# Full-array sums, masks and memory rows with the two attention products apart, and whole accumulators beside the MLP's end, in place of 32-column tiling with adjacent products and single units

## The chip, the core and the metric

The kernel runs on one core of one Trainium2 chip. The core has a matrix engine (TensorE, here PE, with its weight loads listed apart as PEld), VectorE (DVE), ScalarE (ACT), GpSimd (POOL) and SyncE (SP), which issues most DMAs. PE writes only to PSUM, eight banks of 128 x 512 fp32; GpSimd does not read PSUM here. The metric is the device time of one execution in microseconds (us). The kernel before takes 840.97 us (median of 3 runs, 840.32 to 841.74).

## What is computed

`x` is 2048 rows of 512 (bf16). Two branches are mixed by a gate:

```
g = sigmoid((x * gate_w).sum(-1));   out = g * a + (1 - g) * b
b = gelu(layernorm(x) @ w1 + b1) @ w2 + b2            # MLP, 512 -> 1376 -> 512
mem = mem0                                            # 8 rows of 512
for s in range(64):                                   # segments of 32 rows of x
    h = concat([mem, xs])                             # 40 rows
    q, k, v = h @ Wq, h @ Wk, h @ Wv                  # 32 heads of 128
    p = softmax(mask(q @ k.T * scale));  o = (p @ v) @ Wo
    mem, a[s] = o[:8], o[8:]
```

The 8 memory rows that a segment puts out are the first 8 input rows of the next, so the 64 segments are a chain. The other 32 output rows of a segment are not needed by the next one.

## The kernel before, in words

The weights stay in SBUF. First the MLP runs for all 16 tiles of 128 rows: 8 blocks of two tiles, each of 11 chunks of hidden units (88 units `u`); a unit is four 128x256 matmuls (L475) and two 128x512 matmuls (L492) that use the whole 128x128 array. After that comes the loop over 64 segments, four segments (si = 0 to 3) to a tile T.

A segment's 40 rows are split: 32 rows (8 memory rows and 24 rows of x) go through the chain, and the last 8 rows of each of a tile's four segments, the "left" rows, are projected together for a whole tile ahead of time, as side work. Almost every matmul has only 32 rows of output, so four of them are put beside one another in 32-column tiles of the array (`tile_position=(0, 32 * j)`); such a group of four is called a unit here. PE works through a segment in this order, which is the order of the code, since the schedule is manual and every engine takes its instructions in program order:

1. QK: five accumulators in banks of `ring` (L210), 80 matmuls, evacuated by a DVE transpose into `Tt` (L216) and a cast by ACT or POOL (L666).
2. V, first half (L221), then scores (L388, L392) mixed with the second half of V, then the exponentials on ACT (L682, L683).
3. `sums` for the memory rows: a block-diagonal matrix of ones `BO` times E, in 32-column tiles (L365, 8 matmuls). DVE takes the reciprocal (L689) and the product `Pm` (L691).
4. Some units of side work, by `run_fill`.
5. `av` twice (L403, L408), in 32-row tiles of the array (`tile_position=(32 * j, 0)`, 40 matmuls each): the x rows of the segment before (`Px`), and next to it the memory rows of this segment (`Pm`). Both write into the same four banks `U4`.
6. `sums` for the x rows (8 matmuls), one unit of side work, then DVE's second reciprocal (L707).
7. The output projection with Wo (L232) in two halves of 256 columns, 32 matmuls each, into banks `nb` and 6; ACT copies the first half to `wsb`, DVE the second (L727).
8. `mask_mm` for the next segment (L379, 4 matmuls), two units of side work, `mem_out` (L370, 16 matmuls), which transposes the new memory rows, the DVE copy of them into `hT` (L736), and the rest of the side work. Then the next segment's QK, which needs `hT`.

Side work per tile: for si 0 to 2 two accumulators of four units (`left_v`, `left_qk`), for si = 3 `out_units` (two units) and `wo_left` (eight). All side accumulators share bank 5, `out_units` takes bank 6. Evacuations are put into two lists, `act_q` and `dve_q`, and `flush` issues them at set places. `left_qk` is evacuated by an ACT copy into `lt` (L262) and DVE transposes (L266, L270); `out_units` by ACT (L334) and POOL (L335), and SP then issues the output DMA (L336).

For tile 0 the same projections run in `setup()`, beside the last three MLP blocks: the loop over units calls `next(pre, None)` after each unit u, and each call issues one unit of four matmuls.

Of the kernel before, what the change touches and what calls it, by code (L numbers as in the profile page):

```python
# [23 lines left out]
def kernel(ctx, tc, A_x, A_mem0, A_Wq, A_Wk, A_Wv, A_Wo, A_seg_len, B_x, B_w1, B_b1, B_w2, B_b2, gate_w, out):  # L24
    nc = tc.nc
# [149 lines left out]
    pools["nTt"] = 2  # L175

# [18 lines left out]
    def side(shape, dtype=FP32):  # L195
        side_n[0] += 1
        while side_n[0] - 1 in side_todo:
            flush(act_q)
        return bank(5, shape, dtype)
# [52 lines left out]
    def left_qk(T, t, hf):  # L252
# [7 lines left out]
        def ev():  # L260
            lt = pools["sb"].tile([P, 512], BF16, tag="lt", name="lt")
            nc.scalar.copy(out=lt[:], in_=bk[:])  # L262

            def tr():
                if t == 0:
                    nc.vector.transpose(out=QL[T % 2][:, h0:h1, :].rearrange("p h r -> p (h r)"), in_=lt[:])  # L266
                else:
                    for hh in range(h0 // 8, h1 // 8):
                        r0 = 32 * (8 * hh - h0)
                        nc.vector.transpose(out=KL[T % 2][:, :, :, hh, :],  # L270
                                            in_=lt[:, r0:r0 + 256].rearrange("p (g s c) -> p g s c", s=SPT, c=LEFT))
            dve_q.append((None, tr))
        later(act_q, ev, side_k)
        yield

    def left_v(T, vb):
# [7 lines left out]
        def ev():  # L284
            vt = pools["sb"].tile([P, 4, Dh], BF16, tag="lt", name="vt")
# [34 lines left out]
    def out_units(T):  # L320
        ob = bank(6, [P, Dm])
# [7 lines left out]
        o_sb = cw.tile([P, Dm], BF16, tag="o", bufs=1, name="o")  # L329
        if T == NT - 1:  # L330
            nc.vector.scalar_tensor_tensor(out=o_sb[:], in0=ob[:], scalar=g_all[:, T:T + 1], in1=c_all[:, T, :], op0=ALU.mult, op1=ALU.add)
        else:
            of = cw.tile([P, Dm], FP32, tag="Tt", bufs=pools["nTt"], name="of")
            nc.scalar.activation(out=of[:], in_=ob[:], func=ACTF.Copy, scale=g_all[:, T:T + 1])  # L334
            nc.gpsimd.tensor_tensor(out=o_sb[:], in0=of[:], in1=c_all[:, T, :], op=ALU.add)  # L335
        nc.sync.dma_start(out2[T * P:(T + 1) * P, :], o_sb[:])  # L336
# [24 lines left out]

    def sums(o, rhs, start, stop):
        for j in range(4):
            q = slice(32 * j, 32 * j + 32)
            nc.tensor.matmul(o[q], lhsT=BO[:, q], rhs=rhs, start=start, stop=stop, skip_group_check=True, tile_position=(0, 32 * j))  # L365

    def mem_out(aT, wsb):
        for m in range(KC):
            for c in range(4):
                nc.tensor.matmul(aT[32 * c:32 * c + 32, m, :], lhsT=wsb[:, m * P + 32 * c:m * P + 32 * c + 32], rhs=Sel[:, 0:M],  # L370
                                 start=False, stop=True, skip_group_check=True, tile_position=(0, 32 * c))

    def mask_mm():
# [3 lines left out]
        for j in range(4):  # L377
            q = slice(32 * j, 32 * j + 32)
            nc.tensor.matmul(S[q], lhsT=ident[:, q], rhs=MkA[:].unsqueeze(2).to_broadcast([P, 4, 2, EW]),  # L379
                             start=True, stop=True, skip_group_check=True, tile_position=(0, 32 * j))  # L380
# [16 lines left out]
    def av(U, n, s, V, Pt, c_main, c_left, u0, first=True):  # L397

        T, si = divmod(s, SPT)
        for i in range(NG):  # L400
            for j in range(4):
                q = slice(32 * j, 32 * j + 32)
                nc.tensor.matmul(U[j][:, i, :], lhsT=V[q, i, :], rhs=Pt[q, i, c_main:c_main + n],  # L403
                                 start=(first and i == 0), stop=False, skip_group_check=True, tile_position=(32 * j, 0))
# [98 lines left out]
    def setup():  # L503
# [9 lines left out]
        for vb in range(2):  # L513
            yield from left_v(0, vb)
            flush(act_q)
            yield
        for hf in range(2):
            for t in range(2):
                yield from left_qk(0, t, hf)
                flush(act_q)  # L520
                yield
                flush(dve_q)
# [22 lines left out]
    for u in range(NBLK * FC):  # L545
# [34 lines left out]
        if blk >= NBLK - 3:  # L580
# [300 lines left out]
```

## Time and profile before

| what | value |
|---|---|
| median of 3 runs | 840.97 us |
| the profiled execution, its own time | 840.97 us |
| its span, first to last instruction | 839.2 us |
| PE busy | 796.0 us, 95% of the span |
| DVE, ACT, POOL busy | 500.5, 478.8, 246.9 us |
| first QK of segment 0 | 104.37 us |
| first QK of segments 60 and 63 | 780.71 and 813.27 us |
| granted PE clock | 0.999 |

The span is the time from the first to the last instruction; the 1.77 us between it and the execution's time lie outside the instructions. In the timeline a row gives the start and the length in us, then engine, line, operation, output<-inputs, shape and how many instructions are merged. Matmuls overlap, so the distance between the starts of two rows is what a group costs, not its length.

### The profile page before, as it was taken

What the parts mean: (1) busy time and instruction counts of PE and PEld (TensorE: products, weight loads), DVE (VectorE), ACT (ScalarE), POOL (GpSimd) and SP (SyncE); (2) the same over time, 40 slices, a digit from 0 to 9 for tenths busy, and PEclk for the clock granted to TensorE, in tenths of its full rate; (3) what the DMA queues carried; (4) which work ended last, traced back from release to release, by engine and by line L of the source; (5) the groups of instructions that cost most, each with busy time, mean ns of one, the idle gap of its engine ahead of it and who ended that gap; (6) DMA issues with size and microseconds to landing.
All of it is one profiled execution on the core that took longest, in us unless ns stands there. A gap on an engine that the chain in (4) does not pass through costs nothing.

```text
span 839.2 us, 52725 instructions
## 1 busy us (share of the span) xinstructions
PE 796.0 (95%) x24120; PEld 511.4 (61%) x24133; DVE 500.5 (60%) x1036; ACT 478.8 (57%) x1324; POOL 246.9 (29%) x544
## 2 busy tenths in 40 slices
PE   6999989999999999999999999999999999999886
PEld 4665456666666666666666666666666666666554
DVE  5763257565656666665656565656656665656562
ACT  3554556555656556655665565556555556656553
POOL 8000023232333233332323233333233232323321
PEclk9999999999999999999999999999999999999999
DMA  9790300000000010101010100000010101000000
GB/s 320 258 378 26 101 26 14 25 16 15 25 20 26 18 29 10 36 11 36 12 34 5 32 15 23 24 20 27 13 33 11 36 11 33 14 30 4 10 4 24
DMA packets 38230, 37.86 MB, mean 45 GB/s; under 512 B 13545, under 2 KB 36434, under 8 KB 36466
## 3 DMA queue, kind: packets, MB, share of 16 engines
q1 hardware_dynamic: 37874, 34.31, 12.3%
q8 instruction: 190, 3.11, 1.6%
q14 instruction: 38, 0.31, 0.1%
q0 software_dynamic: 128, 0.13, 0.1%
HBM read 26.03 MB, written 6.29 MB: 39 GB/s over the span
## 4 chain that ended last, share of the span: by engine, by line
PE 91%; issue 3%; DVE 2%; DMA 1%; SPq 1%; ACT 1%; POOL 0%; POOLq 0%; DVEq 0%; ACTq 0%
PE b L210 33%; PE b L232 18%; PE b L221 16%; PE b L403 5%; PE hp L475 4%; PE bp L492 4%; PE b L365 3%; PE b L379 2%; PE b L388 2%; PE b L370 1%; PE b L408 1%; DMA Wo_sb<-in_A_x_dram 1%; PE b L392 0%; DVE Tt L216 0%; PE b L323 0%
## 5 line engine op out<-in xcount | busy, mean ns | idle before, releaser
L216 DVE STREAM_TRANSPOSE Tt<-b 128x512 f32<-128x512 f32 (+1 forms) x320 | 180.8, 595 | 77.1 <-PE b L210 63.8
L210 PEld LDWEIGHTS <-hT 128*32 128x32 bf16 x5120 | 133.0, 97 | 106.0 <-DVE hT L736 22.4
L232 PE MATMUL b<-Wo_sb,UTT 128*32 128x256 bf16 (+1 forms) x4736 | 171.6, 285 | 12.5 <-issue 11.9
L232 PEld LDWEIGHTS <-UTT 128*32 128x32 bf16 x4736 | 123.1, 97 | 39.1 <-issue 20.1
L221 PE MATMUL b<-Wv_sb,hT 128*32 128x512 bf16 x2048 | 140.8, 379 | 0.0
L210 PE MATMUL b<-Wq_sb,hT 128*32 128x512 bf16 x2048 | 134.6, 380 | 1.7 <-DVE hT L736 1.6
L210 PE MATMUL b<-Wk_sb,hT 128*32 128x256 bf16 (+1 forms) x3072 | 134.5, 308 | 0.0
L666 ACT CAST KT<-Tt 128x256 bf16<-128x256 f32 (+1 forms) x192 | 87.6, 477 | 49.0 <-DVE Tt L216 48.9
L707 DVE RECIPROCAL R<-b 128x256 f32<-128x256 f32 x64 | 112.5, 1757 | 2.8 <-PE b L365 2.8
L622 POOL TENSOR_TENSOR Px<-E,R 128x256 bf16<-128x256 bf16 x64 | 43.2, 675 | 211.2 <-DVE R L707 211.2
L666 POOL CAST QT<-Tt 128x512 bf16<-128x512 f32 x64 | 39.0, 609 | 220.3 <-DVE Tt L216 220.3
L666 ACT CAST QT<-Tt 128x512 bf16<-128x512 f32 x64 | 39.6, 618 | 81.6 <-DVE Tt L216 81.6
L689 DVE RECIPROCAL R<-b 128x64 f32<-128x64 f32 x64 | 35.7, 557 | 82.2 <-PE b L365 82.2
L631 ACT CAST UTT<-b 128x256 bf16<-128x256 f32 x256 | 78.3, 395 | 6.2 <-PE b L232 6.2
L403 PEld LDWEIGHTS <-V 32*128 32x128 bf16 x4096 | 43.8, 91 | 33.4 <-issue 29.0
L221 PEld LDWEIGHTS <-hT 128*32 128x32 bf16 x2048 | 50.4, 96 | 21.0
L480 ACT ACTIVATE hg<-hp,b_sb 128x256 bf16<-128x256 f32 x80 | 37.7, 473 | 43.0 <-PE hp L475 42.9
L706 ACT CAST UTT<-b 128x64 bf16<-128x64 f32 x128 | 21.0, 215 | 62.9 <-PE b L408 62.7
L475 PE MATMUL hp<-yT,w_sb 128*128 128x256 bf16 (+1 forms) x352 | 54.0, 278 | 2.9 <-ACT hg L480 1.5
L262 ACT CAST lt<-b 128x512 bf16<-128x512 f32 x64 | 37.4, 585 | 32.8 <-PE b L210 13.2
L624 POOL TENSOR_TENSOR racc<-racc,R 128x320 f32<-128x320 f32 x64 | 55.5, 867 | 0.0
L727 ACT CAST wsb<-b 128x256 bf16<-128x256 f32 x66 | 24.6, 372 | 45.2 <-PE b L232 45.2
(113 smaller groups left out, 1134.9 us busy)
## 6 DMA issues: line engine op xcount, KB each, us to landing
Wv_sb<-in_A_Wv_dram SPq DMA_DIRECT2D x4, 1024.0 KB
Wq_sb<-in_A_Wq_dram SPq DMA_DIRECT2D x4, 1024.0 KB
Wk_sb<-in_A_Wk_dram SPq DMA_DIRECT2D x4, 1024.0 KB
Wo_sb<-in_A_Wo_dram SPq DMA_DIRECT2D x2, 2048.0 KB
vd<-vt SPq DMA_DIRECT2D x32, 128.0 KB
vs<-vd SPq DMA_DIRECT2D x256, 16.0 KB
out_dram<-o SPq DMA_DIRECT2D x16, 128.0 KB
Wo_sb<-in_A_x_dram SPq DMA_DIRECT2D x1, 1024.0 KB
```

What stands on the lines that cost most here:

```text
L210: nc.tensor.matmul(bk[32 * j:32 * j + 32, 0:n], lhsT=G[:, kc, :], rhs=W5[t][:, kc, h0:h1, j, :], start=(kc == 0), stop=(kc == KC - 1), til ...
L216: nc.vector.transpose(out=Tt[:, 0:n], in_=bk[:, 0:n])
L221: nc.tensor.matmul(bk[32 * j:32 * j + 32, :], lhsT=G[:, kc, :], rhs=Wv5[:, kc, 4 * vb:4 * vb + 4, j, :], start=(kc == 0), stop=(kc == KC - ...
L232: nc.tensor.matmul(bk[32 * g:32 * g + 32, :], lhsT=ut[:, i, j, c0:c0 + 32], rhs=Wo_sb[:, 4 * i + j, d0:d1], start=(j == 0 and i < 4), stop ...
L403: nc.tensor.matmul(U[j][:, i, :], lhsT=V[q, i, :], rhs=Pt[q, i, c_main:c_main + n], start=(first and i == 0), stop=False, skip_group_check ...
L475: nc.tensor.matmul(hp[:rows, :], lhsT=w1_sb[:, kc, fc * P:fc * P + rows], rhs=yTs[blk][:, kc, :], start=(kc == 0), stop=(kc == KC - 1))
L480: nc.scalar.activation(out=hg_[:rows, :], in_=hp[:rows, :], func=ACTF.Gelu_apprx_tanh, bias=b1_sb[:rows, fc:fc + 1], scale=1.0)
L622: nc.gpsimd.tensor_tensor(out=Px[:, :, 0:32], in0=E[:, :, 16:48], in1=Rr, op=ALU.mult)
L624: nc.gpsimd.tensor_tensor(out=racc[:], in0=racc[:], in1=R[:], op=ALU.add)
L631: nc.scalar.copy(out=UTT[T % 2][:, :, j, c0 + M:c0 + 40], in_=U)
L666: (nc.gpsimd.tensor_copy if bi == 2 else nc.scalar.copy)(out=dst, in_=Tv)
L707: nc.vector.reciprocal(out=R[:, 8 * NG:].rearrange("p (i q) -> p i q", q=32), in_=sr)
```

## The change

- In `setup()` an accumulator's four units are issued at one call, and the MLP's loop makes a call only at every fourth unit u: six accumulators of 16 matmuls in place of 24 calls of 4.
- The `sums`, `mask_mm` and `mem_out` matmuls use the whole array: 2 matmuls for each `sums` (were 8), 1 for the mask (were 4), 4 for `mem_out` (were 16).
- The x rows' product (`av_x`) moves from in front of the memory rows' product to behind the mask, into banks `ne, na, nc_, nb`, where `nb` holds the first half of the output projection until it is evacuated. The memory rows' product has four banks alone.
- `run_fill` is 5 + (si == 3) and then 1 in front of the output projection, and behind it 2 for si == 3 only (were 3 + 2 * (si == 3) + (s == 0), 1, and 2).
- The second half of the output projection goes to bank `nd` instead of 6. DVE copies the first half to `wsb`, ACT the second.
- Side work alternates between two banks, 5 and 6. `left_qk` is transposed by DVE straight from PSUM as fp32 into `Tt`, and POOL casts it; `out_units` is finished by one DVE operation, issued from `dve_q`.

```diff
 def side(shape, dtype=FP32):
     side_n[0] += 1
-    while side_n[0] - 1 in side_todo:
+    n = pools["nside"]
+    while side_n[0] - n in side_todo:
+        flush(dve_q)
         flush(act_q)
-    return bank(5, shape, dtype)
+    return bank(5 + side_n[0] % n, shape, dtype)
...
     def ev():
-        lt = pools["sb"].tile([P, 512], BF16, tag="lt", name="lt")
-        nc.scalar.copy(out=lt[:], in_=bk[:])
...
+        Tv = qk_tr(bk, h0, h1)
+        if t == 0:
+            nc.gpsimd.tensor_copy(out=QL[T % 2][:, h0:h1, :], in_=Tv)
...
-    later(act_q, ev, side_k)
+    later(dve_q, ev, side_k)
...
-    vt = pools["sb"].tile([P, 4, Dh], BF16, tag="lt", name="vt")
+    vt = pools["sb"].tile([P, 4, Dh], BF16, tag="vt", bufs=1, name="vt")
...
-        of = cw.tile([P, Dm], FP32, tag="Tt", bufs=pools["nTt"], name="of")
-        nc.scalar.activation(out=of[:], in_=ob[:], func=ACTF.Copy, scale=g_all[:, T:T + 1])
-        nc.gpsimd.tensor_tensor(out=o_sb[:], in0=of[:], in1=c_all[:, T, :], op=ALU.add)
-    nc.sync.dma_start(out2[T * P:(T + 1) * P, :], o_sb[:])
+    def ev():
+        o_sb = cw.tile([P, Dm], BF16, tag="o", bufs=1, name="o")
         nc.vector.scalar_tensor_tensor(out=o_sb[:], in0=ob[:], scalar=g_all[:, T:T + 1], in1=c_all[:, T, :], op0=ALU.mult, op1=ALU.add)
+        nc.sync.dma_start(out2[T * P:(T + 1) * P, :], o_sb[:])
+    later(dve_q, ev, side_k)
...
-    for j in range(4):
-        q = slice(32 * j, 32 * j + 32)
-        nc.tensor.matmul(S[q], lhsT=ident[:, q], rhs=MkA[:].unsqueeze(2).to_broadcast([P, 4, 2, EW]),
-                         start=True, stop=True, skip_group_check=True, tile_position=(0, 32 * j))
+    nc.tensor.matmul(S, lhsT=ident[:], rhs=MkA[:].unsqueeze(2).to_broadcast([P, 4, 2, EW]), start=True, stop=True, skip_group_check=True)
...
     for hf in range(2):
         for t in range(2):
-            yield from left_qk(0, t, hf)
-            flush(act_q)
+            for _ in left_qk(0, t, hf):
+                pass
+            flush(dve_q)
             yield
...
-    if blk >= NBLK - 3:
+    if blk >= NBLK - 3 and u % 4 == 0:
         next(pre, None)
...
-    ring = (nb, nd, ne, na, nc_)
+    ring = (nd, ne, na, nc_, nb)
...
-    sums(sm, E[:, :, 8:16], True, False)
-    sums(sm, E[:, :, 0:8], False, True)
+    nc.tensor.matmul(sm[:], lhsT=BO[:], rhs=E[:, :, 8:16], start=True, stop=False)
+    nc.tensor.matmul(sm[:], lhsT=BO[:], rhs=E[:, :, 0:8], start=False, stop=True)
     nc.scalar.copy(out=v_out(V, 1), in_=vb1[:])
-    run_fill(3 + 2 * (si == 3) + (s == 0))
+    run_fill(5 + (si == 3))
...
-    U4 = [bank(k, [P, NG * 40]) for k in (nd, ne, na, nc_)]
-    if s >= 1:
-        av(Ux, 32, s - 1, Vs.pop(s - 1), Pxs.pop(s - 1), 0, 32, 24)
-    av(Um, 8, s, V, Pm, 8, 0, 0, first=(s == 0))
+    Um = [bank(k, [P, NG, 8]) for k in (nd, ne, na, nc_)]
+    av(Um, 8, s, V, Pm, 8, 0, 0)
-    sums(sr, E[:, :, 16:48], True, False)
-    sums(sr[:, :, 24:32], E[:, :, 48:56], False, True)
+    nc.tensor.matmul(sr, lhsT=BO[:], rhs=E[:, :, 16:48], start=True, stop=False, skip_group_check=True)
+    nc.tensor.matmul(sr[:, :, 24:32], lhsT=BO[:], rhs=E[:, :, 48:56], start=False, stop=True, skip_group_check=True)
...
-    wp = bank((nb, 6)[half], [P, 256])
+    wp = bank((nb, nd)[half], [P, 256])
...
-    (nc.vector.tensor_copy if half else nc.scalar.copy)(out=wsb[:, d], in_=wp[:])
+    if half == 0:
+        flush(act_q, 2)
+    (nc.scalar.copy if half else nc.vector.tensor_copy)(out=wsb[:, d], in_=wp[:])
 if s + 1 < nseg:
     S_next = mask_mm()
-run_fill(2)
+if live and s >= 1:
+    av_x(s - 1, (ne, na, nc_, nb))
+run_fill(2 * (si == 3))
 if s + 1 < nseg:
-    mem_out(aT, wsb)
+    for m in range(KC):
+        nc.tensor.matmul(aT[:, m, :], lhsT=wsb[:, m * P:(m + 1) * P], rhs=Sel[:, 0:M], start=False, stop=True, skip_group_check=True)
```

## The prediction

> **What bounds the kernel now.** I read the page first (busy shares, queues, chain), then PE's timeline of single segments, then the gaps in it, then the MLP's end. From the page:
>
> ```profile
> PE 796.0 (95%) x24120; PEld 511.4 (61%) x24133; DVE 500.5 (60%) x1036; ACT 478.8 (57%) x1324; POOL 246.9 (29%) x544
> ...
> q8 instruction: 190, 3.11, 1.6%
> ```
>
> PE is busy 95% and carries 91% of the chain of waits; no other engine passes 60%. PE executes 48,253 instructions (24,120 + 24,133), and 190 packets bring instructions: 254 to a packet, some 127 pairs of weight load and matmul. One segment of PE's timeline, si = 2:
>
> ```profile
> 402.43 0.24 PE L365 MATMUL b<-E,BO 128*32 128x64 bf16 x8
> 402.49 0.83 PE L210 MATMUL b<-Wq_sb,GL 128*32 128x512 bf16 x12
> 403.26 0.43 PE L403 MATMUL b<-Px,V 32*128 32x32 bf16 x32
> 403.53 0.23 PE L408 MATMUL b<-Px,VL 32*128 32x32 bf16 x8
> 403.74 0.36 PE L403 MATMUL b<-Pm,V 32*128 32x8 bf16 x32
> 403.94 0.24 PE L408 MATMUL b<-Pm,VL 32*128 32x32 bf16 x8
> 404.11 0.32 PE L365 MATMUL b<-E,BO 128*32 128x256 bf16 x8
> 404.26 0.39 PE L210 MATMUL b<-Wq_sb,GL 128*32 128x512 bf16 x4
> 404.52 1.93 PE L232 MATMUL b<-Wo_sb,UTT 128*32 128x256 bf16 x64
> 406.37 0.37 PE L379 MATMUL b<-MkA,ident 128*32 128x448 bf16 x4
> 406.56 0.69 PE L210 MATMUL b<-Wk_sb,GL 128*32 128x512 bf16 x8
> 406.99 0.27 PE L370 MATMUL b<-Sel,wsb 128*32 128x8 bf16 x13
> ...
> 407.67 1.05 PE L210 MATMUL b<-Wq_sb,hT 128*32 128x512 bf16 x16
> ```
>
> The distance of two starts is a group's cost. Its QK began at 396.89, so the segment took 10.78 us; the next one (si = 3, QK at 418.68) 11.01. The mean is more: QK of the first segment at 104.37 and of the last at 813.27 make 708.9 / 63 = 11.25. The surplus shows in the two segments before these:
>
> ```profile
> 383.06 1.05 PE L232 MATMUL b<-Wo_sb,UTT 128*32 128x256 bf16 x29 [0.50 <-issue]
> ...
> 395.35 0.50 PE L232 MATMUL b<-Wo_sb,UTT 128*32 128x256 bf16 x9 [0.85 <-issue]
> ```
>
> Nothing is waited for, and those segments took 11.40 and 11.74. The gap comes after 35 of the 64 output matmuls, one segment later after 55. A segment has 364 pairs, and 364 + 20 = 3 x 128: the gaps sit where a packet of 128 pairs ends. So PE runs out of instructions where 128 pairs pass too quickly: 128 pairs back from the gaps lie the first and the 20th `av` pair (380.11, about 391.7), and the next packet came 2.95 and 3.65 us later. An unstalled mean of (3 x 10.78 + 11.01) / 4 = 10.84 leaves 0.41 x 63 = 26 us of stalls in the loop, nearly all of this kind.
>
> **The price of a change of tiling.** At the MLP's end single 32-column units stand between whole-array matmuls:
>
> ```profile
> 63.02 0.25 PE L507 MATMUL b<-ident,m 8*128 8x8 bf16 x4
> 63.20 0.61 PE L475 MATMUL hp<-yT,w_sb 128*128 128x256 bf16 x4
> ...
> 65.48 0.40 PE L221 MATMUL b<-Wv_sb,GL 128*32 128x512 bf16 x4
> 65.81 0.61 PE L475 MATMUL hp<-yT,w_sb 128*128 128x256 bf16 x4
> ```
>
> With a unit, L475 recurs after 1.30 us (64.51 to 65.81), without after 0.87 (25.52 to 26.39). The unit itself is 0.217 (L210 x16 at 396.89, next bank at 397.76), so there and back cost 0.215, about 0.12 out of column tiling and 0.10 into it. In the loop: the 12 side matmuls at 402.49 need 0.65 and `av` starts after 0.77, so 0.12; L408 x8 to L365 is 0.17, of which 0.07 is work (eight of L408 at 414.68, the next product at 414.75, with no change between), so 0.10 from row to column tiling. Changes between the whole array and row tiling, three a segment in the new order, do not occur before: bounds 0 and 0.12, and I take the 0.10 of row to column, the nearest row, because both end with the array emptied of a row-tiled product; at 0 the loop would gain 60 x 0.3 = 18 us, which I hold unlikely since every change in the trace costs 0.09 or more.
>
> **The sum, part by part.**
>
> *Setup.* 24 units in 24 calls become six accumulators: 48 changes of tiling become 12. 18 x 0.215 = -3.9 us; PE is dense there (35.74 of 36.00 us busy from 62 to 98), so all of it counts. ACT loses copies there, POOL and DVE have room (1.04 and 11.25 us busy).
>
> *Loop, si = 0 to 2, from the end of V to the start of Wo.* Before: 401.72 to 404.52, 2.80. After: V's last three units 0.65 and a change 0.12; two whole-array `sums`, 0.03 each, and 0.10; five units 1.085 and 0.12; memory product 0.27 (403.26 to 403.53, the product behind a change) and 0.07 + 0.10; second `sums` 0.11 + 0.03 (L475's 256 columns at 0.109) and 0.10; one unit 0.217. Sum 3.03, +0.23. It has two side units more and one product less. The wait for Pm (0.14 before 403.74) is covered by the five units: Pm was ready 1.31 us after the first sum, now PE is there after 1.36. The wait for UTT in front of 404.52 (0.04) is covered too.
>
> *From Wo's end to the next QK.* Before: 406.37 to 407.67, 1.30. After: change 0.12, mask 0.19, change 0.10, `av_x` 0.22 (414.47 to 414.68, product with its loads queued), 0.07 + 0.10, four `mem_out` matmuls, and then `hT`: QK followed the last one by 0.57 (407.10 to 407.67). 0.12 + 0.19 + 0.10 + 0.22 + 0.17 + 0.09 + 0.57 = 1.46, +0.16. The two units behind `mem_out` (0.43) and their change fit in the 0.57. A whole-array 8-column matmul costs about 0.03: four at L507 took 0.18 with the change back.
>
> Together +0.39, 11.17.
>
> *si = 3.* Before 3.10 (412.50 to 415.60) and 1.23 (417.45 to 418.68). After: 3.03 + 0.217 = 3.25, +0.15; behind Wo two units and two further changes go between `av_x` and `mem_out`, and only one unit is left under the 0.57: 1.46 + 0.43 + 0.12 = 2.01, +0.78. Together 11.94.
>
> *Instructions.* A segment falls from 364 pairs to 337 (8 to 2 twice, 4 to 1, 16 to 4), and the two products no longer touch. The quickest 128 pairs were 80 of `av`, 8, 4 and 36 of Wo, 2.4 us. Now: 40, 2, 4, 64, 1 and 17: 0.44 + 0.24 + 0.217 + 1.85 + 0.41 + 0.10 = 3.26, against 2.95 to 3.65 for a packet. Stalls of at most 0.4 remain when a packet starts in the first 25 pairs or so of the memory product: 25 / 128 x 0.2 = 0.04 a segment, bounds 0 and 0.15.
>
> *Total.* 60 segments of tiles 0 to 14 before: 780.71 - 104.37 = 676.3. After: 45 x 11.17 + 15 x 11.94 + 60 x 0.04 = 684.2, less 1.2 since si = 3 of tiles 0 and 1 has less side work (0.74 + 0.43): 683.0, +6.7. Tile 15 has no side work in si 0 to 2, so Pm is waited for (about 11.07 each by the same steps, 10.85 before): +0.7. The tail: the last output must wait for the buffer of the one before (DVE L331 waited 0.76 for that DMA); ACT 0.69 and POOL 1.16 become one DVE operation of 0.75, so that wait goes: -0.8. Sum -3.9 + 6.7 + 0.7 - 0.8 = +2.7. The profiled execution took 840.97, as does the median: 843.7, call it 844.
>
> **What is costed at nothing.** `left_qk`: ACT sheds 64 copies of 0.585, DVE's transposes stay (0.716 for 0.701 and 2 x 0.404), POOL gains a cast not seen before, between 0.61 (its QT cast of the same 128x512) and 1.04 (its VL copy); I take 0.61, the same shape and types. At two in an 11 us segment with some 3.5 of work both fit; behind the first in POOL's order stands the QT cast, due about 2 us later, behind the second `prep_h` and `prep_q`, due in the next segment. Second side bank: the 0.77 and 1.14 PE waits on `vt` in segments 0 and 1 go; they are in the 26. `vt` with one buffer: the second copy waits for the first one's DMA, QT's cast behind it, 1.2 us of room. SP: the output DMA is issued by `flush` a segment later, ahead of nothing that is due. The DVE output operation (0.75) falls before QK's first transpose, where DVE idled 1.16 (before 419.78). `av_x`'s fourth matmul waits for bank `nb`, so for DVE's first `wsb` copy behind the 1.76 reciprocal: that ended at 406.32, copy 0.42, so free 0.42-0.44 after Wo's end; PE is there after 0.42. No cover at all: each 0.1 more is 6 us.
>
> **The skill against the rows.** The page "Runtime: NRT & Kernel Launch", section "Instruction fetch mechanics", calls crossing a 16 KiB block mostly hidden. The gaps of 0.50 and 0.85 say otherwise here; by the page nothing would be regained, and my sum would end near 868. "TensorE: Matmul & The Clock Gate", section "LDWEIGHTS", gives columns / 1.2 ns, 107 ns for 128 columns, and speaks against whole-array `mem_out` and `sums` (an estimate from the page: eight loads, some +0.5 us a segment, 32 us and 876); the L507 row with 128 columns shows about 0.03 each, so the row decides.
>
> **Rivals.**
> 1. *Faster.* Changes of tiling behind a small matmul are cheaper than behind a 512-column one; the nearest row is L507's 0.18 for four matmuls and the change back, so 0.09 to 0.10. The loop gains about 7.25 changes a segment; at 0.09 instead of 0.11 that is 464 x 0.02 = -9, 835. It decides below 0.10. Chance 0.27.
> 2. *Packets still late.* If a packet needs 3.65 wherever the memory product opens it, or 128 pairs pass quicker than I count, 0.15 to 0.2 a segment: +8, 852. For it: 3.26 lies inside 2.95 to 3.65. Chance 0.16.
> 3. *The memory row's chain.* `nb` or `wsb` late by 0.1 to 0.15, with no side units to cover: +8, 852. For it: a margin near 0. Chance 0.14.
> 4. *POOL late with QT or KL*, scores wait 0.3: 862. Against: 29% busy. Chance 0.05.
>
> **How the numbers follow.** The forecast has 0.38. About what a measurement can tell here is 0.2%, 1.7 us. The forecast's own spread is the products' 0.21 to 0.30 (two a segment, -4 to +5) and the packets' 0 to 0.15: 839 to 850, so it gives 0.03 to faster, 0.13 to same, 0.22 to slower. Rival 1 gives 0.25 faster, 0.02 same. Rivals 2 to 4 are slower, but for 0.02 same. Faster 0.28, same 0.17, slower 0.55. Range: from rival 1 with a point more of it, 833, to rivals 2 or 3 with part of the other, 856.
>
> **What the profile after would show.** Right: whole accumulators of 0.87 us beside the MLP and first QK near 100.5; segments near 11.2 and 11.9 with little spread; few "issue" gaps in PE; `av_x` behind the mask without a wait. Wrong: L403 waiting on DVE's `wsb`, L370 on `wsb`, L388 on QT from POOL; "issue" gaps of 0.5 still there; or segments under 11.0, which would say that I overprice the changes.

## The result and the profile after

The changed kernel takes 835.08 us (median of 4 runs, 834.65 to 835.76). The kernel before took 841.36 us beside it (840.32 to 843.19), so the ratio is 0.9924, with a 95% interval of 0.9905 to 0.9943. In a later set of runs it was 0.9895 (0.9872 to 0.9918), a little below the 0.991 to 0.994 expected of it. The change is a gain of about 0.8 to 1%. The forecast was 844, a small loss: its range held the time, its likeliest case and its sign were wrong.

The profiled execution took 834.65 us with a span of 832.9. Cut at the first QK of segment 0 and of segment 63, the spans of the two kernels compare like this:

| stretch | before | after | difference | forecast |
|---|---|---|---|---|
| start to first QK (MLP and `setup`) | 104.37 | 100.40 | -3.97 | -3.9 |
| QK of segment 0 to QK of segment 60 (tiles 0 to 14) | 676.3 | 673.4 | -2.9 | +6.7 |
| QK of segment 60 to QK of segment 63 | 32.56 | 32.54 | 0.0 | +0.7 |
| QK of segment 63 to the end | 25.93 | 26.58 | +0.65 | -0.8 |

Setup came as forecast. The loop did not get slower, and the tail did not get shorter. From the page after:

```profile
PE 804.7 (97%) x22405; PEld 495.4 (59%) x22417; DVE 501.7 (60%) x1019; ACT 434.0 (52%) x1245; POOL 273.7 (33%) x625
```

PE issues 1,715 matmuls fewer and yet is busy 8.7 us longer, in a span 6.3 us shorter: idle time of PE was turned into work and then some of it was saved. Which idle time it was, the list of PE's waits tells (what was waited for, us in total, times, longest). Before:

```profile
PE b L232 <- issue: 11.9, 22, 0.9
```

After:

```profile
PE b L384 <- DVE Pm L679: 5.7, 6, 1.3
...
PE b L384 <- issue: 0.5, 2, 0.3
PE b L719 <- issue: 0.2, 1, 0.2
```

"Issue" is time in which nothing that the profile shows was waited for; the prediction read it as packets of instructions that come late. All rows of it come to 16.1 us before and to 0.7 after. The list takes only part of the late time, as will be seen from the segments, but the direction is plain. One segment after (si = 1; the prediction showed si = 2 of before, which has the same number of side units), from the end of V to the next QK:

```profile
385.58 0.82 PE L222 MATMUL b<-Wv_sb,hT 128*32 128x512 bf16 x12
386.33 0.20 PE L673 MATMUL b<-E,BO 128*128 128x64 bf16 x1
386.37 0.19 PE L674 MATMUL b<-E,BO 128*128 128x64 bf16 x1
386.49 1.05 PE L211 MATMUL b<-Wq_sb,GL 128*32 128x512 bf16 x16
387.37 0.39 PE L211 MATMUL b<-Wk_sb,GL 128*32 128x512 bf16 x4
387.69 0.36 PE L384 MATMUL b<-Pm,V 32*128 32x8 bf16 x32
387.90 0.23 PE L389 MATMUL b<-Pm,VL 32*128 32x32 bf16 x8
388.06 0.28 PE L684 MATMUL b<-E,BO 128*128 128x256 bf16 x1
388.18 0.19 PE L685 MATMUL b<-E,BO 128*128 128x64 bf16 x1
388.31 0.40 PE L211 MATMUL b<-Wk_sb,GL 128*32 128x512 bf16 x4
388.53 1.92 PE L233 MATMUL b<-Wo_sb,UTT 128*32 128x256 bf16 x64
390.38 0.36 PE L360 MATMUL b<-MkA,ident 128*128 128x448 bf16 x1
390.68 0.37 PE L384 MATMUL b<-Px,V 32*128 32x32 bf16 x32
390.89 0.24 PE L389 MATMUL b<-Px,VL 32*128 32x32 bf16 x8
391.07 0.26 PE L719 MATMUL b<-Sel,wsb 128*128 128x8 bf16 x4
391.25 0.61 PE L211 MATMUL b<-Wk_sb,GL 128*32 128x512 bf16 x8
391.69 0.61 PE L211 MATMUL b<-Wq_sb,hT 128*32 128x512 bf16 x8
```

The order is the one described, there is no wait in it, and the distances of the starts are the costs. This segment began at 380.75 and took 10.94 us. All segments, and the sums in them, are taken apart below.

The MLP's end shows whole accumulators: 16 matmuls of L222 with the change of tiling behind them, 0.98 us from 67.76 to 68.74 (0.87 and 0.12 by the prediction's rows).

```profile
67.76 1.05 PE L222 MATMUL b<-Wv_sb,GL 128*32 128x512 bf16 x16
68.74 0.61 PE L456 MATMUL hp<-yT,w_sb 128*128 128x256 bf16 x4
```

### The profile page after: what moved, and what is told of

It reads as the page before. It is cut to its first block, busy times and chain, and to the rows that moved or that the text cites. A ratio compares the mean times of both kernels' runs of the same rounds, so it can differ in the third digit from the quotient of the medians.

```text
span 832.9 us, 49239 instructions
## 1 busy us (share of the span) xinstructions
PE 804.7 (97%) x22405; PEld 495.4 (59%) x22417; DVE 501.7 (60%) x1019; ACT 434.0 (52%) x1245; POOL 273.7 (33%) x625
## 4 chain that ended last, share of the span: by engine, by line
PE 93%; DVE 3%; DMA 1%; issue 1%; SPq 1%; ACT 1%; DVEq 0%; ACTq 0%
PE b L211 35%; PE b L233 18%; PE b L222 17%; PE b L384 5%; PE hp L456 4%; PE bp L473 4%; PE b L360 2%; PE b L369 2%; PE b L684 2%; PE b L719 1%; PE b L389 1%; PE b L673 1%; DMA Wo_sb<-in_A_x_dram 1%; PE b L320 1%; PE b L373 0%
## 5 line engine op out<-in xcount | busy, mean ns | idle before, releaser
L217 DVE STREAM_TRANSPOSE Tt<-b 128x512 f32<-128x512 f32 (+1 forms) x384 | 225.6, 613 | 85.5 <-PE b L211 71.8
L233 PE MATMUL b<-Wo_sb,UTT 128*32 128x256 bf16 (+1 forms) x4736 | 162.7, 285 | 1.2 <-ACT UTT L619 0.8
L222 PE MATMUL b<-Wv_sb,hT 128*32 128x512 bf16 x2048 | 141.9, 379 | 0.0
L211 PE MATMUL b<-Wq_sb,hT 128*32 128x512 bf16 x2048 | 132.9, 380 | 1.4 <-DVE hT L720 1.4
L233 PEld LDWEIGHTS <-UTT 128*32 128x32 bf16 x4736 | 121.4, 97 | 19.1 <-ACT UTT L619 1.5
L384 PEld LDWEIGHTS <-V 32*128 32x128 bf16 x4096 | 35.3, 91 | 46.2 <-DVE Pm L679 32.0
L222 PEld LDWEIGHTS <-hT 128*32 128x32 bf16 x2048 | 49.5, 96 | 21.1
L720 DVE CAST hT<-b 128x32 bf16<-128x32 f32 x63 | 12.1, 191 | 62.4 <-PE b L719 61.6
```

Source lines behind the costliest of these rows:

```text
L211: nc.tensor.matmul(bk[32 * j:32 * j + 32, 0:n], lhsT=G[:, kc, :], rhs=W5[t][:, kc, h0:h1, j, :], start=(kc == 0), stop=(kc == KC - 1), til ...
L217: nc.vector.transpose(out=Tt[:, 0:n], in_=bk[:, 0:n])
L222: nc.tensor.matmul(bk[32 * j:32 * j + 32, :], lhsT=G[:, kc, :], rhs=Wv5[:, kc, 4 * vb:4 * vb + 4, j, :], start=(kc == 0), stop=(kc == KC - ...
L233: nc.tensor.matmul(bk[32 * g:32 * g + 32, :], lhsT=ut[:, i, j, c0:c0 + 32], rhs=Wo_sb[:, 4 * i + j, d0:d1], start=(j == 0 and i < 4), stop ...
```

## The experiments

### How the segments are read

For each kernel the distance from one segment's first QK matmul to the next one's was taken from the trace, in tiles 0 to 14. "Undisturbed" is the mean over si = 0 to 3 of the shortest segment of that kind from tile 2 on (tiles 0 and 1 have less side work in si = 3); in the changed kernel most segments lie within 0.04 us of the shortest of their kind, and its medians of the four kinds agree to 0.01 us in two profiled executions. "Rest" is the mean of all 60 segments less the undisturbed one: late packets, and the waits of the first tile. The kernel before took 839.39 to 845.48 us in the different sets of runs; ratios are to the kernel before run beside the same kernels.

| kernel | us | ratio (95%) | mean | undisturbed | rest |
|---|---|---|---|---|---|
| before | 841.36 | 1 | 11.27 | 10.81 | 0.46 |
| before, setup alone | 835.21 | 0.9956 (0.9941 to 0.9972) | 11.24 | 10.85 | 0.39 |
| before, whole-array matmuls alone | 846.31 | 1.0016 (1.0000 to 1.0033) | 11.38 | 11.12 | 0.26 |
| after, column tiling kept | 839.66 | 0.9926 (0.9897 to 0.9954) | 11.32 | 11.03 | 0.29 |
| after | 835.08 | 0.9924 (0.9905 to 0.9943) | 11.22 | 11.15 | 0.07 |
| before, 20 matmuls of padding, place A | 878.13 | 1.0396 (1.0373 to 1.0420) | 11.82 | | |
| before, 20 matmuls of padding, place B | 869.00 | 1.0288 (1.0265 to 1.0311) | 11.71 | | |
| after, units dealt as before | 854.94 | 1.0119 (1.0088 to 1.0150) | 11.56 | 11.50 | 0.06 |
| after, no units behind the mask | 832.22 | 0.9918 (0.9898 to 0.9939) | 11.17 | 11.10 | 0.08 |
| after, left Q and K by ACT | 830.02 | 0.9892 (0.9871 to 0.9913) | 11.14 | 11.11 | 0.03 |
| mixed | 827.98 | 0.9874 (0.9853 to 0.9895) | 11.08 | 10.96 | 0.12 |
| after, again | 835.79 | 0.9895 (0.9872 to 0.9918) | 11.24 | 11.16 | 0.07 |
| mixed, again | 829.21 | 0.9820 (0.9792 to 0.9847) | 11.12 | 10.96 | 0.16 |
| mixed, left Q and K by ACT | 823.76 | 0.9753 (0.9726 to 0.9780) | 11.03 | 10.89 | 0.14 |

The last three lines are from one chip, beside "after, units dealt as before". Where two variants are compared with each other below, the text says whether they shared a chip.

That the rest is late packets can be read from the traces. Number PE's matmuls from the first QK of segment 0, and take for each what its distance to the one before exceeds the median at that place of the segments of the same kind. If packets of 128 pairs come late, the excess stands at matmuls that lie a multiple of 128 apart. It does: in the kernel before, one of the 128 possible remainders (35) carries 28.4 us of the 31.7 us found in tiles 0 to 14, and 0.46 x 60 is 27.6. Such a sum is 12.3 us with the whole-array matmuls alone, 16.1 with column tiling kept in the new kernel, 1.9 in the changed kernel, and 4.3 to 7.7 in the mixed ones below.

### The setup alone

```diff
-            yield from left_v(0, vb)
+            for _ in left_v(0, vb):
+                pass
...
-                yield from left_qk(0, t, hf)
+                for _ in left_qk(0, t, hf):
+                    pass
...
-        if blk >= NBLK - 3:
+        if blk >= NBLK - 3 and u % 4 == 0:
```

> The kernel before with the change of the setup alone: the six accumulators of tile 0 are issued whole, at every fourth unit of the MLP's end. Evacuations and the loop stay as they were. 18 pairs of changes of tiling fewer at 0.215: 3.9 us less, ratio 0.9953, first QK 4.0 us earlier. Rival (the MLP's end had room, or the evacuations were the cause): less than 1.5 us.

Measured: 0.9956, that is 3.7 us of 841, with the first QK at 101.03 in place of 104.37, 3.3 us earlier for the 4.0 expected (the changed kernel's stands at 100.40 and, in the later runs, at 100.78). So 0.44% of the change's 0.76% is the setup, and the price of a change of tiling there (0.215 for both) holds to about a fifth. About 0.3% is left for the loop and the tail.

### The whole-array matmuls alone, and the order alone

Two kernels make a square with the ones given. One is the kernel before, with only `sums`, `mask_mm` and `mem_out` turned to the whole array (the two products stay adjacent, setup stays as it was):

```diff
-        for j in range(4):
-            q = slice(32 * j, 32 * j + 32)
-            nc.tensor.matmul(o[q], lhsT=BO[:, q], rhs=rhs, start=start, stop=stop, skip_group_check=True, tile_position=(0, 32 * j))
+        nc.tensor.matmul(o, lhsT=BO[:], rhs=rhs, start=start, stop=stop, skip_group_check=True)
```

and likewise for the mask and `mem_out`.

> The kernel before, with nothing changed but the sums, the mask and the memory rows, which use the whole array (337 pairs a segment, not 364); the two attention products stay adjacent and the side work stays as it was. Theory (changes of tiling cost about 0.11 each, and fewer instructions mean fewer late packets): five to seven changes more add 0.35 to 0.45 us to an undisturbed segment (10.84 to about 11.2), and the stalls fall from 0.38 to 0.1 a segment, so 841 to 849 us. Rival, changes are cheap and the late packets have nothing to do with it: 835 or less if a change is nearly free, about 866 if changes cost 0.11 and the stalls stay.

The other is the changed kernel with these three put back into column tiling, the mask and `mem_out` in the same way as the sums:

```diff
-            nc.tensor.matmul(sm[:], lhsT=BO[:], rhs=E[:, :, 8:16], start=True, stop=False)
-            nc.tensor.matmul(sm[:], lhsT=BO[:], rhs=E[:, :, 0:8], start=False, stop=True)
+            sums(sm, E[:, :, 8:16], True, False)
+            sums(sm, E[:, :, 0:8], False, True)
...
-                nc.tensor.matmul(aT[:, m, :], lhsT=wsb[:, m * P:(m + 1) * P], rhs=Sel[:, 0:M], start=False, stop=True, skip_group_check=True)
+            mem_out(aT, wsb)
```

> The changed kernel, with sums, mask and memory rows back in 32-column tiling (364 pairs a segment, not 337); the products stay apart, setup and side work as changed. Theory: undisturbed segments fall from 11.16 to about 10.85, but with 364 pairs packets come late again (0.15 to 0.25 us a segment), so 826 to 833 us. Without the link to the number of instructions: all of the five changes saved, 0.3 x 64 = 19 us, 816. If changes are cheap in the loop: 834 to 836.

Measured: 1.0016 and 0.9926. The first, 846.31 us, lies in the 841 to 849 expected. The second, 839.66 us on a chip where the kernel before took 845.48, misses its 826 to 833: its undisturbed segment was expected at 10.85 and is 11.03, and its rest is 0.29, for late packets of 0.15 to 0.25 expected.

The whole array costs between nothing and 0.3% without the new order, and with it the two tilings give 0.9924 and 0.9926 (not on one chip). In the segments the price is there: the undisturbed segment grows by 0.31 us (10.81 to 11.12) in the old order, and by 0.12 (11.03 to 11.15) in the new one. There the groups themselves cost 0.31 more too (si = 1: the end of V and the first sums 0.14, the second sums 0.09, `mem_out` 0.08), but in column tiling PE arrives earlier and loses 0.19 of it: the step to the memory rows' product takes 0.06 longer, the one to Wo 0.04, the one to the next QK 0.09. The price is given back by the rest: that falls by 0.20 (0.46 to 0.26) and by 0.22 (0.29 to 0.07). Neither the new kernel in column tiling (0.29) nor the shorter program in the old order (0.26) brings the late packets down to 0.07; both together do. The new kernel differs from the old by more than the order (side banks, evacuations, the dealing of side units), so its share is not the order's alone.

Where a late packet is left in the new kernel with column tiling, it often stands in the product behind the mask, as here:

```profile
390.19 1.93 PE L233 MATMUL b<-Wo_sb,UTT 128*32 128x256 bf16 x64
392.03 0.37 PE L373 MATMUL b<-MkA,ident 128*32 128x448 bf16 x4
392.34 0.30 PE L397 MATMUL b<-Px,V 32*128 32x32 bf16 x20
393.29 0.24 PE L397 MATMUL b<-Px,V 32*128 32x32 bf16 x12 [0.65 <-issue]
```

These lines also settle a term of the forecast. From Wo to a mask in column tiling, with no change between, it is 1.84 us here. From Wo to a mask on the whole array, with a change between, it is 1.85 in the changed kernel (388.53 to 390.38 above), and 1.86 in the kernel with only the whole-array matmuls:

```profile
396.96 1.92 PE L232 MATMUL b<-Wo_sb,UTT 128*32 128x256 bf16 x64
398.82 0.36 PE L373 MATMUL b<-MkA,ident 128*128 128x448 bf16 x1
399.11 0.62 PE L210 MATMUL b<-Wk_sb,GL 128*32 128x512 bf16 x8
```

The 64 output matmuls go in 16 rounds of 0.109, which is 1.75. Some 0.1 us is empty ahead of the mask in either tiling, and the change of tiling disappears in it. What makes that time empty is not settled; it is not the change alone, since it is there without one. The change behind the mask is paid: mask to unit is 0.29 in these lines, 0.19 in column tiling.

### Padding: do packets run late?

If PE's instructions come in packets of 128 pairs of weight load and matmul, a segment of exactly 3 x 128 pairs puts the ends of the packets at the same places in every segment. Two kernels fill every segment of the kernel before up to 384 pairs with tiny matmuls into an unused corner of the mask's bank (their sums are read by nothing). They differ in the number of such matmuls ahead of the loop, 26 or 66, which moves the places.

```diff
+    def pad(B, n):
+        for i in range(n):
+            c = i % 4
+            nc.tensor.matmul(B[32 * c:32 * c + 32, 480:488], lhsT=BO[:, 32 * c:32 * c + 32], rhs=Sel[:, 0:M],
+                             start=False, stop=True, skip_group_check=True, tile_position=(0, 32 * c))
+    pad(S_next[0], 26)
...
+            if n_seg >= 320:
+                pad(S_next[0], 384 - n_seg)
```

> The kernel before with tiny matmuls into unused columns behind the mask, so that every segment has exactly 384 = 3 x 128 pairs, and 26 of them ahead of the loop. The padding costs at most 0.13 us a segment (8 us). The place of the packet's ends in a segment no longer moves: here at pairs 9, 137 and 265 of a segment. Theory (stalls come from packets that end too soon after the last): few stalls, segments of 10.85 to 11.0 all alike, 825 to 838 us. Rival (stalls come from elsewhere, DMA traffic or semaphores): 841 to 849, and the same as the other padding.

> The same padding with 66 instead of 26 tiny matmuls ahead of the loop (0.3 us more work), so that packets end at pairs 97, 225 and 353. Theory: the packet from 97 to 225 or the one after it is passed in well under 3.5 us in every segment, so nearly every segment stalls by 0.6 to 0.9 us, 860 to 885 us. Rival: the same time as the other padding within 1 us.

Measured: +3.96% and +2.88%, 878.13 and 869.00 us. Place B lies in the 860 to 885 us expected. Place A was thought to be the harmless one and is the worse one, a clear miss: where a packet ends harmlessly was not understood. Where it ends was. The expectations named pairs 9, 137 and 265 for place A and 97, 225 and 353 for place B before the kernels ran, and PE has a gap of more than 0.1 us right behind pair 265 in 58 of 63 segments of A and right behind pair 353 in 55 of 63 of B. From A to B the place moves by 40 modulo 128 (353 + 40 = 265 + 128), the number of matmuls that B has more ahead of the loop, and the remainder 35 of the unpadded kernel becomes 9 and 97 when 26 and 66 stand ahead (35 - 26, and 35 - 66 + 128); a wait for data or for another engine would stay with its instruction. In place B, two successive segments:

```profile
397.21 0.29 PE L614 MATMUL b<-Sel,BO 128*32 128x8 bf16 x20
397.34 0.38 PE L221 MATMUL b<-Wv_sb,GL 128*32 128x512 bf16 x1
398.28 0.61 PE L221 MATMUL b<-Wv_sb,GL 128*32 128x512 bf16 x7 [0.57 <-issue]
...
409.05 0.29 PE L614 MATMUL b<-Sel,BO 128*32 128x8 bf16 x20
409.17 0.38 PE L210 MATMUL b<-Wk_sb,GL 128*32 128x512 bf16 x1
410.34 0.61 PE L210 MATMUL b<-Wk_sb,GL 128*32 128x512 bf16 x7 [0.80 <-issue]
```

The 20 matmuls themselves take 0.12 us, some 7.5 us in the loop, and the kernel loses 24 and 33. The gap stands in both segments behind the same matmul, the first of eight side matmuls, which is pair 353. No segment of place B with eight side units is shorter than 11.23 us, three packets of 3.74, though its instructions need 10.81 + 0.12 = 10.93. A segment before holds 364 pairs, 2.84 packets in 10.81 us undisturbed or 3.80 each, next to what the padded ones reach; one after holds 337, 2.63 packets in 11.15 us or 4.24 each, with half a microsecond a packet to spare.

The page "Runtime: NRT & Kernel Launch", section "Instruction fetch mechanics", of the Trainium skill calls the cost of crossing a block mostly hidden. It is hidden in the changed kernel (0.7 us of issue waits) and is not in the padded ones; the measurement decides, and by these figures the cost is hidden here only where 128 pairs take longer to execute than the next packet takes to come.

### The side units ahead of the product

The changed kernel with the units dealt out as before:

```diff
-            run_fill(5 + (si == 3))
+            run_fill(3 + 2 * (si == 3) + (s == 0))
...
-        run_fill(2 * (si == 3))
+        run_fill(2)
```

> The changed kernel with the side units dealt out as before: three ahead of the memory rows' product, one, then two behind the mask product and two at the end. Theory (five units ahead of the product are what covers the chain of sum, reciprocal and Pm): from the first sum, Pm is ready after 1.18 us in the changed kernel, and with two units of 0.217 fewer PE arrives after about 0.93, so it waits about 0.25 to 0.4; the two units between two changes of tiling add one change of about 0.11. Together 0.35 to 0.5 in 48 segments, 17 to 24 us: ratio 1.011 to 1.021, and waits of PE for Pm in the trace. Rival (the order of the units is indifferent, and what the changed kernel gains behind the setup comes from the second side bank): only the changes, 0.11 to 0.2 a segment, 5 to 10 us, ratio 0.998 to 1.004 and no wait for Pm.

Measured: 854.94 against 835.79 of the changed kernel on the same chip, +19.2 us. The waits say where:

```profile
PE b L384 <- DVE Pm L679: 19.0, 49, 1.1
```

In the changed kernel this row reads 5.7 us in 6 waits. In the timeline the product starts 1.23 us after the start of the three units, and 0.40 of that is waiting:

```profile
405.74 0.83 PE L211 MATMUL b<-Wq_sb,GL 128*32 128x512 bf16 x12
406.97 0.36 PE L384 MATMUL b<-Pm,V 32*128 32x8 bf16 x32 [0.40 <-DVE Pm L679]
```

The theory's 17 to 24 us and its wait are met, the rival (the order of the units is indifferent) gave 5 to 10. With the products apart, side units cover the chain from the first sum over DVE's reciprocal to `Pm`; five of them do, but for a few hundredths of a microsecond in si = 2 (see the last experiment).

### The units behind the mask, and a mixed kernel

For si = 3 the changed kernel puts two units between two changes of tiling, which the forecast held for its worst place. Without them (they run at the segment's end):

```diff
-        run_fill(2 * (si == 3))
```

> The changed kernel without the two units of side work between the x rows' product and the memory rows in every fourth segment; they are issued behind the memory rows instead, where hT is waited for. Two changes of tiling fewer (0.2) and a wait for hT covered (about 0.1 of it) in 16 segments: 4 to 5 us less than the changed kernel, about 0.987 of the kernel before. Rival (PE is filled either way): no more than 1 us.

Measured: 0.9918 against the 0.9924 of the changed kernel, on different chips, so the ratio shows no gain and misses the expected one. The segments do: si = 3 falls from 11.67 to 11.43, 0.24 x 15 = 3.6 us, and the others stay.

The mixed kernel takes the cheaper tiling at each place: `sums` and mask in column tiling, next to units in column tiling; `mem_out` on the whole array; no units behind the mask.

```diff
+            sums(sm, E[:, :, 8:16], True, False)
+            sums(sm, E[:, :, 0:8], False, True)
...
+        for j in range(4):
+            q = slice(32 * j, 32 * j + 32)
+            nc.tensor.matmul(S[q], lhsT=ident[:, q], rhs=MkA[:].unsqueeze(2).to_broadcast([P, 4, 2, EW]),
+                             start=True, stop=True, skip_group_check=True, tile_position=(0, 32 * j))
...
-        run_fill(2 * (si == 3))
```

> The changed kernel with both sums and the mask in 32-column tiling, the memory rows with the whole array, and without the two units between the x rows' product and the memory rows. Four changes of tiling fewer than in the changed kernel for 15 pairs more (352 a segment). Theory: undisturbed segments 10.75 to 10.85 and late packets of 0.1 to 0.2 a segment: 12 us less than the changed kernel on average, 5 to 16, ratio 0.973 to 0.987. If late packets take back all of it, as they do with 364 pairs: 0.990 or more.

> The mixed kernel once more (sums and mask in column tiling, memory rows by the whole array, no units behind the mask product): 0.9874 before, so 0.985 to 0.990, and 0.5% below the changed kernel on the same chip.

Measured: 0.9874, just outside the 0.973 to 0.987 expected, and on the second chip 0.9820, below the 0.985 to 0.990 expected and 6.6 us (0.8%, for 0.5%) below the changed kernel there. In the profiled executions the four kinds of segment fall from 11.01, 10.94, 11.03, 11.67 to 10.85, 10.79, 10.98, 11.23, which is 12 us over 15 tiles; some 5 of them go back to late packets (rest 0.07 to 0.16), since it has 352 pairs in most segments and not 337.

### Who evacuates the left rows' Q and K

The second segment of the changed kernel takes 12.53 us and not 11. PE waits there for `Pm`:

```profile
119.98 0.36 PE L384 MATMUL b<-Pm,V 32*128 32x8 bf16 x32 [1.26 <-DVE Pm L679]
```

and DVE's timeline shows what was ahead of the reciprocal, a transpose of `left_qk` as fp32, which itself waited 2.70 us for PE:

```profile
118.37 0.72 DVE L217 STREAM_TRANSPOSE Tt<-b 128x512 f32<-128x512 f32 x1 [2.70 <-PE b L211]
119.01 0.52 DVE L677 RECIPROCAL R<-b 128x64 f32<-128x64 f32 x1
```

The next kernel is the changed one with `left_qk` as before: an ACT copy to bf16 and DVE transposes out of SBUF (and with it `vt` back in the buffers of `lt`).

```diff
-            Tv = qk_tr(bk, h0, h1)
...
-        later(dve_q, ev, side_k)
+            lt = pools["sb"].tile([P, 512], BF16, tag="lt", name="lt")
+            nc.scalar.copy(out=lt[:], in_=bk[:])
+            def tr():
+                if t == 0:
+                    nc.vector.transpose(out=QL[T % 2][:, h0:h1, :].rearrange("p h r -> p (h r)"), in_=lt[:])
...
+            dve_q.append((None, tr))
+        later(act_q, ev, side_k)
```

> The changed kernel with the left_qk accumulators evacuated as before, by an ACT copy and DVE transposes, in place of a DVE transpose and a POOL cast (two side banks stay). Theory (ACT, DVE and POOL lie beside PE): the same within 0.2%. Rival (part of the gain came from relieving ACT): slower by 2 us or more.

Measured: 0.9892, where no difference to 0.9924 was expected, and the second segment at 11.20. As the two had not shared a chip, the same edit was made to the mixed kernel and run beside it:

> The mixed kernel with the left rows' Q and K evacuated by ACT, and transposed by DVE from bf16, as in the kernel before. Theory (the fp32 transposes at the head of DVE's list delay Pm in single segments, most in the second one, 12.26 us here and 12.53 in the changed kernel against 11.20 with ACT's copies, and by 0.05 to 0.1 in others): 1.3 us less in tile 0 and up to 2 to 4 us in the rest, so 0.2 to 0.6% below the mixed kernel, ratio 0.982 to 0.986. Rival (the difference of the two kernels that were not compared side by side lay between chips or in where the packets fall): within 0.2% of the mixed kernel but for the second segment.

Measured: 823.76 against 829.21, 5.4 us or 0.66% faster on the same chip, a little more than the 0.2 to 0.6% expected. The traces agree (694.0 against 699.4 us from the first QK to the last): 1.5 us in the first two segments, 0.18 in each undisturbed segment of si = 2, 0.05 in each of si = 3. In si = 2 the product stands further behind the mixed kernel's fifth unit:

```profile
395.18 0.75 POOL L268 CAST KL<-Tt 128x256 bf16<-128x256 f32 x2 [0.81 <-DVE Tt L217]
395.87 1.04 POOL L299 COPY VL<-vs 128x1024 bf16<-128x1024 bf16 x1
395.96 0.56 DVE L690 RECIPROCAL R<-b 128x64 f32<-128x64 f32 x1 [0.85 <-PE b L359]
396.59 0.40 PE L211 MATMUL b<-Wk_sb,GL 128*32 128x512 bf16 x4
396.63 0.43 DVE L692 TENSOR_TENSOR Pm<-E,R 128x128 bf16<-128x128 bf16 x1
396.86 0.35 POOL L247 COPY GL<-xT 128x128 bf16<-128x128 bf16 x1
397.11 0.36 PE L397 MATMUL b<-Pm,V 32*128 32x8 bf16 x32
```

0.52 us between the starts, against 0.39 with ACT's copies (393.58 to 393.97):

```profile
392.96 0.56 DVE L696 RECIPROCAL R<-b 128x64 f32<-128x64 f32 x1 [0.97 <-PE b L364]
393.58 0.40 PE L211 MATMUL b<-Wk_sb,GL 128*32 128x512 bf16 x4
393.62 0.29 DVE L698 TENSOR_TENSOR Pm<-E,R 128x128 bf16<-128x128 bf16 x1
393.97 0.36 PE L402 MATMUL b<-Pm,V 32*128 32x8 bf16 x32
```

So the expectation's reason holds for the second segment only. In si = 2 no transpose stands ahead of the reciprocal: DVE waits for PE's sum in both kernels. What differs is `Pm` itself, 0.43 us beside POOL's copies of `VL` and `GL` and 0.29 without them, 0.14 of the 0.18; the new cast of `KL` on POOL is what pushes these copies back to it. In the changed kernel's trace too `Pm` takes 0.40 or 0.41 in 13 of the 16 segments of si = 2, each time beside the copy of `VL`, and 0.29 in every segment of the other three kinds. No run moves the copies alone, so that they slow DVE is read from the overlap.

This kernel, 823.76 us or 0.9753 of the kernel before on its chip and 0.9856 of the changed one, is the best that was run.

## Why the prediction was wrong

**What held.** *Setup*: -3.97 for -3.9. *The price of a change of tiling*: in the segment shown the first sums with their change take 0.16 (forecast 0.16), the second 0.25 (0.24), the mask 0.30 (0.29), the products' left rows with the change to the whole array 0.16 and 0.18 (0.17). So the 0.10 that was only taken from its nearest row, between the whole array and row tiling, holds. *Packets*: 0.07 a segment are left, the first tile's waits in it, and 0.03 by the count of 128 above, for a forecast of 0.04. *Covers*: the five units cover `Pm` in the steady segments but for si = 2, `av_x` follows the mask without a wait, and four whole-array `mem_out` matmuls cost 0.18 with the change, not four loads of 0.107.

**The step that failed** is the loop's sum, 11.17 and 11.94 a segment. Measured on undisturbed segments it is 11.01, 10.94, 11.03 and 11.67. In the segment shown, 10.94, these terms were too large:
- *"change 0.12" from Wo's end to the mask*: nothing is paid there (0.01 in the square of kernels). The forecast took Wo's length from a row that ended in an empty 0.1 and put the change on top of it. This is half of the error: 0.12 of 0.23.
- *"memory product 0.27 (403.26 to 403.53, the product behind a change)"*: 0.21 (387.69 to 387.90). Before, one of the two adjacent products took 0.27 and the other 0.21, the x rows' in the row that was used and the memory rows' in si = 3 (414.75 to 415.02); standing alone, both take 0.21. The price of a product next to another was carried over to one that stands alone. Why one of two adjacent ones takes longer was not looked into.
- *"QK followed the last one by 0.57"*: from the start of `mem_out` to QK it is 0.62, for 0.66 forecast (0.09 + 0.57); `mem_out` with its change (0.18) and two units (0.44) make it up, not `hT`.
- The rest is 0.02 in V's last units.

In us: 45 segments x 0.177 = -8.0, 15 x 0.27 = -4.0. Against that stand +2.4 for late packets and the first tile's waits: 4.8 in all for 2.4 forecast, 1.6 of it in the second segment. The credit of 1.2 for less side work in tiles 0 and 1 came (1.1). That is -9.5 on tiles 0 to 14, where +6.7 was forecast and -2.9 measured. *Tile 15*: 0.0 for +0.7 (segments of 10.84 for 11.07). With the setup's -0.07 and the tail's +1.45, 843.7 becomes 834.9, for 834.65 measured.

**The tail** had the wrong sign, +0.65 for -0.8. The wait for the output DMA went, as forecast: DVE's two output operations start as soon as their matmuls end. But the end did not come sooner for it: from PE's last matmul to the end of the span it is 6.20 us before (833.00 to 839.2) and 6.66 after (826.22 to 832.9). What sets these last microseconds was not taken apart. And PE now waits for ACT's copies of the last x rows' product. Before and after:

```profile
825.26 3.91 PE L232 MATMUL b<-Wo_sb,UTT 128*32 128x256 bf16 x128
826.37 0.37 ACT L727 CAST wsb<-b 128x256 bf16<-128x256 f32 x1 [1.83 <-PE b L232]
826.64 1.20 ACT L631 CAST UTT<-b 128x256 bf16<-128x256 f32 x4
```

```profile
820.29 0.37 ACT L708 CAST wsb<-b 128x256 bf16<-128x256 f32 x1 [1.73 <-PE b L233]
820.56 1.21 ACT L619 CAST UTT<-b 128x256 bf16<-128x256 f32 x4
821.00 2.11 PE L233 MATMUL b<-Wo_sb,UTT 128*32 128x256 bf16 x64 [0.75 <-ACT UTT L619]
```

In ACT's order the copies into `UTT` stand behind its copy into `wsb`. Before, that was the first half of the projection, and the copies ran beside the second half. Now it is the second half, and they start when Wo has ended, which costs 0.75. The swap of the two `wsb` copies was not costed for the tail. Against it a late packet of 0.67 went.

**The rivals.** Rival 1 gave 835, and the time is 835.08, but that is luck, its reason is not what happened: it had every change behind a small matmul at 0.09 in place of 0.11. They cost what the forecast said; one change, behind Wo, is free, and another term was too large. Rival 2 (late packets) can be excluded, rival 3 (`nb` or `wsb` late) shows nowhere in the steady segments. Rival 4 (POOL late with QT or KL) does not either; what did cost something is next to it, `left_qk` moved from ACT to DVE and POOL, which was costed at nothing. It was argued from the busy share and from the room in a segment, not from what stands behind it: in the second segment the reciprocal for `Pm` behind a transpose on DVE (1.26 us), and in si = 2 POOL's copies, which now run beside `Pm` (0.40 for 0.29).

**How near the sign was.** The loop's result is the difference of two terms of some 20 us: the undisturbed segment grows by 0.34 us (10.81 to 11.15), 60 times, and the rest falls by 0.39. The forecast had both, and missed the first by 0.2 us a segment.

## What to carry to other kernels

Where PE is the bound and waits for nothing, look at the gaps that the profile calls issue and count the instructions between them: here segments with little more than 3.7 us for 128 pairs ran into late packets, and 20 needless tiny matmuls cost three to more than four times their own time. Whether late instructions are the cause is tested by adding matmuls ahead of the loop: the gaps must move by their number. A price taken from the distance of two rows holds whatever stands between them: before a new cost is added behind a row, see whether the row ended in an empty stretch that would swallow it. And an operation moved to an engine with room must be looked up in that engine's order: ask what stands behind it, whether it will wait for something late, and what will then run at the same time.

## What the runs showed of the hardware

- A change of tiling cost PE about 0.09 to 0.12 us in each direction, between column tiling, row tiling and the whole array. The page "TensorEngine Tiling (Array Packing)", section "Key Properties", of the Trainium skill says that a change of mode drains the array, which agrees; the number is from these runs. Behind Wo and ahead of the mask it cost 0.01; there 0.1 us is empty in either tiling.
- Instructions came to PE 128 pairs at a time: in segments of 384 pairs the gap stays at one place (pair 265 or 353, as named beforehand), no such segment with its eight side units was shorter than 11.23 us, and in the kernel before 28.4 us of late time stand a multiple of 128 matmuls apart. Where the packets end moved the time of otherwise equal kernels by 9 us (878.1 and 869.0).
- Undisturbed segments of the mixed kernel were the same to 0.02 us on two chips (medians 10.85, 10.81, 10.98, 11.23 and 10.85, 10.83, 10.99, 11.23); what differed is the late part (rest 0.12 and 0.16).
- The same DVE product (`Pm`, 128x128 bf16) took 0.29 us alone and, in most segments, 0.40 to 0.43 beside POOL's copies of `VL` and `GL`.
